# A linear-attention and token-mixer block: when one tile of h is normalised, and in what order GpSimd works

## The chip, the cores and the metric

The kernel runs on one core of one Trainium2 chip. The metric is the device time of one execution in microseconds (us), here 528.55 us as the median of three runs (527.94 to 528.89). Shorter is better. Engine names: TensorE (PE, matmuls and transposes; PEld is its weight load), VectorE (DVE), ScalarE (ACT), GpSimd (POOL) and SyncE (SP, which issues most DMAs).

## The reference

One sequence of S = 2048 tokens with D = 512 channels goes through two residual blocks. The first is a linear attention with 32 heads of 16 channels, the second a token-mixing MLP with F = 1792 hidden units.

```python
def _A_ref(x, wqkv, w_phi, wo):
    qkv = ((x @ wqkv).reshape(B, S, 3, H, Dh)).transpose(2, 0, 3, 1, 4)
    q, k, v = qkv[0], qkv[1], qkv[2]
    pq = einsum("bhsd,hdf->bhsf", q, w_phi)          # the same for pk
    phi_q = concatenate([softmax(pq), softmax(-pq)], -1)
    kv  = einsum("bhsf,bhsd->bhfd", phi_k, v);  z = einsum("bhsf->bhf", phi_k)
    num = einsum("bhqf,bhfd->bhqd", phi_q, kv)
    den = einsum("bhqf,bhf->bhq", phi_q, z)[..., None] + 1e-6
    return (num / den).transpose(0, 2, 1, 3).reshape(B, S, D) @ wo

def _B_ref(x, w1, b1, w2, b2):
    h = _layernorm(x)
    u = gelu(einsum("bsd,sf->bdf", h, w1) + b1)      # over the token axis
    return (einsum("bdf,fs->bds", u, w2) + b2).transpose(0, 2, 1)

h  = x + _A_ref(_layernorm(x), A_wqkv, A_w_phi, A_wo)
h2 = h + _B_ref(_layernorm(h), B_w1, B_b1, B_w2, B_b2)
```

## The kernel before

The tokens are cut into NT = 16 tiles of 128. Every large product is made of three fp32r matmuls (`mm3`, lines 63 to 67): high part by high part (L65), high by the low part of the moving operand (L66), low part of the weight by high (L67). So each operand is split into a high part, which ScalarE copies, and a low part, which a second engine subtracts (`split`, L58: copy at L60, subtraction at L61).

Up to about 140 us of the profile the keys, values and the sums over all tokens are made. Then comes the attention stage, the loop `for it in range(NT + 3)`. It is a software pipeline over the tiles: in iteration it each step works on a tile of its own. For PE, DVE, ACT and POOL the order of the instructions is the order in which the loop writes them, and each engine works its queue strictly in that order; SyncE's queue is ordered by a planner. The steps:

- `s_pq(t)` (GpSimd, L465): the product of the 128x1024 tile of query features with its weights; written in iteration t-1. TensorE's transposes of tile t need it.
- `s_ez(t)` (GpSimd, L447): the product ez of the features with the summed keys, in iteration t-3. `s_den` (VectorE, L456 to L462) makes the weights of the product from it.
- `negate` (GpSimd, L164, L165): the second half of a tile's logits, for ten tiles; the last of them comes around 182 us.
- `q_exp` (ScalarE, L176): the exponentials of a tile.
- `s_tr(t)` (TensorE, L532): eight transposes of tile t in iteration t; ScalarE copies them (`pht`, L534). There is one PSUM tile `tn` for them.
- `s_num(j)` (TensorE, L551): in even iterations, the numerator of the pair of tiles j = it/2-1 from `pht`, into the same `tn`; ScalarE copies its high part (`oh`, L557), VectorE subtracts the low part (`ol`, L562).
- `s_wo(t)` (TensorE): 12 matmuls into the single PSUM tile `po`, in iteration t+2. In even iterations it stands ahead of the transposes, in odd ones behind.
- `s_h(t)` (VectorE, L579): h = x + po and its row sums, at the end of iteration t+2; a DMA writes h out.
- `s_moments(t)` (ScalarE, L585 to L587): mean and variance of h, in iteration t+3.
- `s_rstd(t)` (GpSimd, L590 and L591): the root r2 = variance^-0.5 and then -mean times r2; in iteration t+3.
- `s_hn(t)` (ScalarE L595 and L60, GpSimd L61): the normalised tile hn = h * r2 + bias, its high part, and on GpSimd the low part of `hs`.
- `fill(p)` (TensorE, 6 matmuls `pu<-hs`): the MLP's first product for one tile of tokens and 256 hidden units. In iteration it it uses tile it-6 for p = 1, then tile it-5 for p = 0 (LAG = 5). Its weights are streamed: SyncE loads `wraw`, ScalarE makes `whi` (L614), VectorE `wlo` (L606, in `flush`).

`s_hn` is written in even iterations only, for two tiles: for tile it-4 near the head of the iteration, ahead of the exponentials and of `s_moments`, and for tile it-3 as the iteration's last step, behind `s_rstd(it-3)` of the same iteration.

After the loop come the rest of the MLP's first product (up to about 383 us) and its second product, both ordered for TensorE; from 255 us to the last product TensorE has no idle time in the profile.

Of the kernel before, what the change touches and what calls it, by code (L numbers as in the profile page):

```python
# [11 lines left out]
AF = mybir.ActivationFunctionType  # L12
# [7 lines left out]
NT = S // P  # L20
# [16 lines left out]
def block_kernel(ctx: ExitStack, tc: tile.TileContext, x, xT, wT, phic, wo, w1, b1, w2, b2,  # L37
                 kvmask, ident_in, out):
    nc = tc.nc
# [12 lines left out]
    r2 = cst.tile([P, NT], F32, name="r2")  # L52
# [5 lines left out]
    def split(hi, lo, src, lo_engine):  # L58

        nc.scalar.activation(hi, src, AF.Copy)  # L60
        lo_engine.tensor_sub(lo, src, hi)  # L61
# [98 lines left out]
    def negate():  # L160

        if MN:
            ev, mx, mn = MN.pop(0)
            nc.gpsimd.tensor_sub(mn, mn, mx)  # L164
            nc.gpsimd.tensor_sub(ev[:, :, 1], mn.unsqueeze(3).to_broadcast([P, NPR, 2, DH]), ev[:, :, 0])  # L165
# [5 lines left out]
    def run(*lists):  # L171
        for op in turns(*lists):
            op()
# [192 lines left out]
    def q_mm():  # L366
        if q["mm"] < NT:
            PS[q["mm"]] = proj(q["mm"], wqh, wql, ps_q, "pu")
            q["mm"] += 1

    def q_logits(lag):
        n = q["logits"]
        if n < min(NT, q["mm"] - lag + NT * (q["mm"] == NT)):
            EQ[n] = big.tile([P, NG, P], F32, name="eq", tag="big")
            q["logits"] += 1
            return logit_ops(PS[n], EQ[n], n >= len(Q_AT))
        return []

    def q_exp(lag):
        n = q["exp"]  # L380
        if n < min(NT, q["logits"] - len(MN) - lag):
            exps(n, EQ[n])
            q["exp"] += 1

    def q_sums(lag):
        n = q["sum"]
        if n < min(NT, q["exp"] - lag + NT * (q["exp"] == NT)):
            q["sum"] += 1
            return q_sum(n)
        return []  # L390
# [54 lines left out]
    def s_ez(t):  # L445
        EZ[t] = az.tile([P, NG, P], F32, name="ez")
        nc.gpsimd.tensor_mul(EZ[t], EQ[t], zB)  # L447

    def s_den(t):


        tz = az.tile([P, NPR, 2, 2], F32, name="tz")
        den = az.tile([P, NPR, 2], F32, name="den")
        W[t] = az.tile([P, NPR, 2, 2], F32, name="w", bufs=3)
        other = SQ[t]
        return [lambda: nc.vector.reduce_sum(tz.rearrange("p g c h -> p (g c h)"), heads(EZ[t]), axis=AX.X),  # L456
                lambda: nc.vector.scalar_tensor_tensor(tz[:, :, 0], other[:, :, 1], 1e-6, tz[:, :, 0],
                                                       op0=ALU.mult, op1=ALU.add),
                lambda: nc.vector.tensor_mul(tz, other, tz),
                lambda: nc.vector.reduce_sum(den, tz.rearrange("p g c h -> p g h c"), axis=AX.X),  # L460
                lambda: nc.vector.reciprocal(den, den),
                lambda: nc.vector.tensor_mul(W[t], other, den.unsqueeze(2).to_broadcast([P, NPR, 2, 2]))]  # L462

    def s_pq(t):
        nc.gpsimd.tensor_mul(heads(EQ[t]), heads(EQ[t]), W[t].rearrange("p g c h -> p (g c h)").unsqueeze(2).to_broadcast([P, 2 * H, DH]))  # L465
# [58 lines left out]
    HN, HT, PHT, OS, PO, VE = {}, {}, {}, {}, {}, {}  # L524

    def s_tr(t):
        j, i = divmod(t, 2)
        if i == 0:
            PHT[j] = ak.tile([P, NG, 2, P], F32, name="pht", bufs=1)
        ptr = ps_t.tile([P, 2, 4, P], F32, name="tn")  # L530
        for g in range(NG):
            nc.tensor.transpose(ptr[:, g // 4, g % 4, :], EQ[t][:, g, :], ident)  # L532
        for half in range(2):
            nc.scalar.activation(PHT[j][:, half * 4:half * 4 + 4, i, :], ptr[:, half], AF.Copy)  # L534

    def s_kv():

        pt = ps_o.tile([P, 2, P], F32, name="po")
        for b in range(2):
            nc.tensor.transpose(pt[:, b, :], kvS[:, 2 * b:2 * b + 2, :].rearrange("p n f -> p (n f)"), ident)  # L540
        nc.scalar.activation(kvB, pt, AF.Copy)

    def s_num(j):


        pn = ps_t.tile([P, 2, 4, P], F32, name="tn")
        for b in range(2):
            for c in range(4):
                for r in range(2):
                    rows, cols = slice(64 * r, 64 * r + 64), slice(32 * c, 32 * c + 32)  # L550
                    nc.tensor.matmul(pn[cols, r, 2 * b:2 * b + 2, :], kvB[rows, b, cols], PHT[j][rows, 4 * b + c, :, :],  # L551
                                     start=True, stop=True, skip_group_check=True)
        oh = ak.tile([P, 2, 2, 2, P], F32R, name="oh", bufs=1)
        ol = ak.tile([P, 2, 2, 2, P], F32R, name="ol", bufs=1)
        pv = pn.rearrange("p r (b i) s -> p i r b s", i=2)
        for i in range(2):
            nc.scalar.activation(oh[:, i], pv[:, i], AF.Copy)  # L557
        OS[j] = oh, ol, pv

    def s_ol(j):  # L560
        oh, ol, pv = OS[j]
        return [lambda i=i: nc.vector.tensor_sub(ol[:, i], pv[:, i], oh[:, i]) for i in range(2)]  # L562

    def s_wo(t):
        oh, ol, _ = OS[t // 2]
        i = t % 2
        PO[t] = po = ps_o.tile([P, D], F32, name="po")
        for j in range(4):
            mm3(po, oh[:, i, j // 2, j % 2, :], ol[:, i, j // 2, j % 2, :], woh[:, j, :], wol[:, j, :], j == 0, j == 3)

    def s_x(t):
        HT[t] = ak.tile([P, D], F32, name="h", bufs=4)
        nc.sync.dma_start(HT[t], x[t * P:(t + 1) * P, :])
# [8 lines left out]
    def s_moments(t):  # L582

        junk = ak.tile([P, D], F32, name="hj", bufs=1)
        nc.scalar.activation(VE[t][:, 1:2], VE[t][:, 2:3], AF.Copy, scale=-1.0 / D)  # L585
        nc.scalar.activation(junk, HT[t], AF.Square, bias=VE[t][:, 1:2], accum_out=VE[t][:, 3:4])
        nc.scalar.activation(VE[t][:, 0:1], VE[t][:, 3:4], AF.Identity, scale=(1.0 + EPS) / D, bias=eps2)  # L587

    def s_rstd(t):
        nc.gpsimd.tensor_tensor(r2[:, t:t + 1], VE[t][:, 0:1], mhalf[:, :1], op=ALU.pow)  # L590
        nc.gpsimd.tensor_mul(VE[t][:, 1:2], VE[t][:, 1:2], r2[:, t:t + 1])  # L591

    def s_hn(t):
        hn = ak.tile([P, D], F32, name="hn")
        nc.scalar.activation(hn, HT[t], AF.Identity, scale=r2[:, t:t + 1], bias=VE[t][:, 1:2])  # L595
        HN[t] = big.tile([P, 2, D], F32R, name="hs", tag="big")
        split(HN[t][:, 0], HN[t][:, 1], hn, nc.gpsimd)
# [5 lines left out]
    def flush():  # L603
        while LATER:
            wl_, raw, wh_ = LATER.pop(0)
            LO.append(nc.vector.tensor_sub(wl_, raw, wh_).ins)  # L606
# [35 lines left out]
    def fills(it):  # L642
        if FN[1] < it - LAG:
            fill(1, ps_q)
        if FN[0] <= it - LAG:
            fill(0, ps_f)

    for it in range(NT + 3):
        even = it % 2 == 0
        if 0 <= it + 1 < NT:  # L650
            s_pq(it + 1)
        if it == 0:
            s_tr(0)
            s_kv()
        if it == 1:
            run(q_logits(0))
            q_mm()
            s_tr(1)
        if it > 1 and even:
            if it <= NT:  # L660
                s_num(it // 2 - 1)
            if it >= 4:
                s_hn(it - 4)
        den = s_den(it + 2) if it + 2 < NT else []
        if it > 1 and even and it <= NT:
            ol = s_ol(it // 2 - 1)
            run(ol[:1] + den[:1] + ol[1:])
            den = den[1:]
        if it < NT:
            s_x(it)  # L670
        if it + 3 < NT:
            s_ez(it + 3)
        negate()
        q_mm()
        fills(it)
        q_exp(0)
        logits = q_logits(1)
        if it >= 3 and even:
            s_moments(it - 3)
        if it > 1 and even and it - 2 < NT:  # L680
            s_wo(it - 2)
        if 1 < it < NT:
            s_tr(it)
        if it > 1 and not even and it - 2 < NT:
            s_wo(it - 2)
        if it >= 3 and not even:
            s_moments(it - 3)
        if it >= 3:
            s_rstd(it - 3)
        run(logits + (q_sums(0) if it > 0 else []), den)  # L690
        flush()
        if 0 <= it - 2 < NT:
            s_h(it - 2)
        if it > 0:
            negate()
        if it >= 3 and even:
            s_hn(it - 3)
        for p in range(2):
            if it >= LAG - 3 + p and FL[p] <= FN[p] + 2 * (FN[p] > 0):
                fill_load(p)  # L700
# [139 lines left out]
    for n, (sp, p) in enumerate(STEPS):  # L840
        t = 2 * sp
# [118 lines left out]
```

## Time and profile before

| | |
|---|---|
| median of three runs | 528.55 us (527.94 to 528.89) |
| the profiled execution's own time | 527.88 us |
| its span, first to last instruction | 526.1 us |
| what lies around the span | 1.78 us |
| granted TensorE clock | 0.999 |
| busy: PE, PEld, DVE, ACT, POOL | 98%, 83%, 75%, 53%, 47% of the span |
| attention stage | about 140 to 256 us |

A row of the timeline gives the start and the duration in us, the engine, the source line, out<-in, and in brackets how long the engine was idle before it and which instruction ended the wait. Rows of repeated instructions are merged (x8). A row of the waits gives the total in us, the number of times, and the longest. A row of the windows gives a stretch and each engine's busy time in it, with the number of instructions in brackets. Durations on PE include the pipeline's depth: neighbouring matmuls overlap, so TensorE's pace is read from the distance of starts.

### The profile page before, as it was taken

The page shows a single profiled execution, that of the slowest core. Times are in us where ns is not written, and L with a number is a line of the kernel's source. Part 1 is how long each engine was busy: PE and PEld are TensorE (multiplying, and loading weights), DVE is VectorE, ACT ScalarE, POOL GpSimd, SP SyncE. Part 2 cuts the span into 40 slices and gives each one's busy share as a digit, 9 for nine tenths or more (in the row PEclk, how much of TensorE's full clock was granted, in tenths as well). Part 3 has the DMA queues.
Part 4 walks back from the last instruction along what each step waited for, and adds up shares of the span by engine and source line. Part 5 has one row for each costly group of instructions (what it writes and reads, how often), then busy time and mean ns, then how long its engine had stood idle before and what let it go on. Part 6 is the DMA issues. An engine that isn't in the chain of part 4 may idle for free.

```text
span 526.1 us, 8910 instructions
## 1 busy us (share of the span) xinstructions
PE 516.9 (98%) x3379; PEld 436.5 (83%) x3379; DVE 394.0 (75%) x681; ACT 277.7 (53%) x480; POOL 245.2 (47%) x204
## 2 busy tenths in 40 slices
PE   9999999999999979999999999999999999999997
PEld 8888888887877757777788888888889999999997
DVE  6893999976899989874426423824869889888985
ACT  6999843534247676557757422625553424444430
POOL 2589699985999988897425000000002122211210
PEclk9999999999999999999999999999999999999999
DMA  8634210020122233334234345532114686667733
GB/s 307 205 120 121 83 40 21 1 87 17 56 86 80 82 103 118 104 119 130 91 101 120 92 143 169 175 104 82 60 61 109 161 191 150 137 153 190 162 44 78
DMA packets 36298, 58.52 MB, mean 111 GB/s; under 512 B 3744, under 2 KB 19360, under 8 KB 36256
## 3 DMA queue, kind: packets, MB, share of 16 engines
q1 hardware_dynamic: 31936, 51.37, 30.4%
q0 software_dynamic: 4032, 6.42, 8.8%
q8 instruction: 26, 0.43, 0.3%
q10 hardware_dynamic: 288, 0.17, 0.1%
q14 instruction: 16, 0.13, 0.1%
HBM read 46.81 MB, written 11.14 MB: 110 GB/s over the span
## 4 chain that ended last, share of the span: by engine, by line
PE 82%; POOL 12%; DVE 3%; ACT 2%; issue 0%; POOLq 0%; ACTq 0%
PE py L822 11%; PE pu L65 11%; PE pu L66 10%; PE pu L67 10%; PE py L826 10%; PE py L823 6%; POOL ez L447 4%; POOL eq L465 3%; PE pv L66 3%; PE pv L67 3%; PE pv L65 3%; PE pk_ps L65 2%; PE pk_ps L66 2%; PE pk_ps L67 2%; POOL hs L61 2%; PE kvp L212 2%
## 5 line engine op out<-in xcount | busy, mean ns | idle before, releaser
L606 DVE TENSOR_TENSOR wlo<-wraw,whi 128x512 fp32r<-128x512 f32 x56 | 50.9, 912 | 56.2 <-ACT whi L614 56.0
L65 PE MATMUL pu<-hs,whi 128*128 128x512 f32 x224 | 87.2, 395 | 0.0
L66 PE MATMUL pu<-hs,whi 128*128 128x512 f32 x224 | 87.1, 389 | 0.0
L67 PE MATMUL pu<-hs,wlo 128*128 128x512 f32 x224 | 87.1, 390 | 0.0
L881 POOL DMA_DIRECT2D out<-ot x7 | 6.2, 889 | 157.3 <-DVE ot L877 157.3
L795 ACT ACTIVATE whi<-wraw 128x1792 fp32r<-128x1792 f32 x28 | 47.5, 1701 | 46.6 <-PE py L822 20.6
L804 DVE TENSOR_TENSOR wlo<-wraw,whi 128x1792 fp32r<-128x1792 f32 x28 | 56.5, 2022 | 12.5 <-PE py L823 8.9
L822 PE MATMUL py<-uf,whi 128*128 128x512 f32 x175 | 63.4, 399 | 0.0
L614 ACT ACTIVATE whi<-wraw 128x512 fp32r<-128x512 f32 x56 | 34.9, 626 | 50.3 <-PE pu L66 46.0
L65 PEld LDWEIGHTS pu<-hs,whi 128*128 128x128 f32 x224 | 42.1, 188 | 10.8 <-issue 2.5
L67 PEld LDWEIGHTS pu<-hs,wlo 128*128 128x128 f32 x224 | 42.1, 188 | 9.0 <-DVE wlo L606 0.4
L823 PE MATMUL py<-uf,wlo 128*128 128x256 f32 x175 | 49.2, 281 | 0.0
L66 PEld LDWEIGHTS pu<-hs,whi 128*128 128x128 f32 x224 | 42.1, 188 | 8.5
L447 POOL TENSOR_TENSOR ez<-eq,zB 128x1024 f32<-128x1024 f32 x16 | 40.6, 2539 | 4.4 <-ACT zB L494 4.4
L826 PE MATMUL py<-uf,whi 128*128 128x256 f32 x210 | 39.0, 283 | 0.0
L822 PEld LDWEIGHTS py<-uf,whi 128*128 128x128 f32 x175 | 33.0, 188 | 6.8
L200 POOL TENSOR_TENSOR pk<-pk,sk 128x1024 f32<-128x1024 f32 x16 | 31.0, 1940 | 7.6 <-DVE sk L199 5.0
L826 PEld LDWEIGHTS py<-uf,whi 128*128 128x128 f32 x210 | 32.4, 189 | 1.4
L823 PEld LDWEIGHTS py<-uf,wlo 128*128 128x128 f32 x175 | 33.1, 189 | 0.0
L465 POOL TENSOR_TENSOR eq<-eq,w 128x1024 f32<-128x1024 f32 x16 | 31.9, 1996 | 1.2 <-DVE w L462 1.2
L204 POOL TENSOR_TENSOR zacc<-zacc,pk 128x1024 f32<-128x1024 f32 x13 | 31.2, 2402 | 0.5
L61 POOL TENSOR_TENSOR hs<-hn,hs 128x512 fp32r<-128x512 f32 x16 | 21.4, 1340 | 17.9 <-ACT hs L60 17.9
(179 smaller groups left out, 1329.2 us busy)
## 6 DMA issues: line engine op xcount, KB each, us to landing
wraw<-in_w SPq DMA_DIRECT2D x56, 256.0 KB, 2.8
wraw<-in_w SPq DMA_DIRECT2D x28, 512.0 KB, 4.1
xraw<-in_xT SPq DMA_DIRECT2D x16, 256.0 KB, 2.9
xh<-in_x SPq DMA_DIRECT2D x16, 256.0 KB, 2.6
h<-in_x SPq DMA_DIRECT2D x16, 256.0 KB, 2.7
out<-h SPq DMA_DIRECT2D x16, 256.0 KB, 3.0
out<-ot POOLq DMA_DIRECT2D x14, 256.0 KB, 4.5
wraw<-in_wT SPq DMA_DIRECT2D x12, 256.0 KB, 4.9
```

The costliest lines, as they stand in the source:

```text
L65: nc.tensor.matmul(o, ah, bh, start=first, stop=False)
L66: nc.tensor.matmul(o, ah, bl, start=False, stop=False)
L67: nc.tensor.matmul(o, al, bh, start=False, stop=last)
L447: nc.gpsimd.tensor_mul(EZ[t], EQ[t], zB)
L465: nc.gpsimd.tensor_mul(heads(EQ[t]), heads(EQ[t]), W[t].rearrange("p g c h -> p (g c h)").unsqueeze(2).to_broadcast([P, 2 * H, DH]))
L606: LO.append(nc.vector.tensor_sub(wl_, raw, wh_).ins)
L614: nc.scalar.activation(wh_, raw, AF.Copy)
L795: nc.scalar.activation(WH[g], RAW[g], AF.Copy)
L804: nc.vector.tensor_sub(wl_, RAW[g], WH[g])
L822: nc.tensor.matmul(o, a[0], b, start=start, stop=stop, skip_group_check=True)
L823: nc.tensor.matmul(o[:, 0], a[1], b[:, 0], start=False, stop=stop, skip_group_check=True)
L826: nc.tensor.matmul(o[:, half], a[x], b[:, y], start=start and first and i == 0, stop=stop and i == 2, skip_group_check=True)
```

## The change

Four things are rewritten in the loop of the attention stage.

1. `s_hn` is written once in every iteration, always for tile it-4. On ScalarE it stands behind the exponentials and ahead of `s_moments(it-3)`; in odd iterations it stands behind `s_tr(it)`, so behind ScalarE's copies of the transposes. The loop has one more iteration (it = 19), in which tile 15 is normalised.
2. On GpSimd an iteration's order becomes product, ez, (negate), low part, root, (negate). Before, the low part stood ahead of ez for tile it-4, and at the end of the iteration, behind the root, for tile it-3.
3. The product of -mean and r2 (L591 on GpSimd) becomes an ACTIVATE of ScalarE on 128x1 elements, in front of hn.
4. While logits are still being made, `flush` (VectorE's `wlo`) stands behind `s_h` instead of ahead of it. Later it stays ahead.

The loads of h (`s_x`, four buffers) now wait for the later `s_hn` on ScalarE, and the planner puts SyncE's queue in a slightly different order. TensorE's matmuls are the same in number and, up to 13 tiles, in order; the last two fills of the loop are written in the added iteration.

```diff
     def s_rstd(t):
         nc.gpsimd.tensor_tensor(r2[:, t:t + 1], VE[t][:, 0:1], mhalf[:, :1], op=ALU.pow)
-        nc.gpsimd.tensor_mul(VE[t][:, 1:2], VE[t][:, 1:2], r2[:, t:t + 1])
 
     def s_hn(t):
+        nc.scalar.activation(VE[t][:, 1:2], VE[t][:, 1:2], AF.Copy, scale=r2[:, t:t + 1])
         hn = ak.tile([P, D], F32, name="hn")
...
-    for it in range(NT + 3):
+    for it in range(NT + 4):
...
-        if it > 1 and even:
-            if it <= NT:
-                s_num(it // 2 - 1)
-            if it >= 4:
-                s_hn(it - 4)
+        if it > 1 and even and it <= NT:
+            s_num(it // 2 - 1)
...
         logits = q_logits(1)
-        if it >= 3 and even:
+        if it >= 4 and even:
+            s_hn(it - 4)
+        if 3 <= it < NT + 3 and even:
             s_moments(it - 3)
...
-        if it >= 3 and not even:
+        if it >= 4 and not even:
+            s_hn(it - 4)
+        if 3 <= it < NT + 3 and not even:
             s_moments(it - 3)
-        if it >= 3:
+        if 3 <= it < NT + 3:
             s_rstd(it - 3)
         run(logits + (q_sums(0) if it > 0 else []), den)
-        flush()
+        if it > 0:
+            negate()
+        if not logits:
+            flush()
         if 0 <= it - 2 < NT:
             s_h(it - 2)
-        if it > 0:
-            negate()
-        if it >= 3 and even:
-            s_hn(it - 3)
+        flush()
```

## The prediction

> **What bounds the kernel now.** I read the page first, then TensorE's windows, then the waits of the attention stage, then the timeline of each engine around the places where TensorE stands still. The page:
>
> ```profile
> span 526.1 us, 8910 instructions
> PE 516.9 (98%) x3379; PEld 436.5 (83%) x3379; DVE 394.0 (75%) x681; ACT 277.7 (53%) x480; POOL 245.2 (47%) x204
> PE 82%; POOL 12%; DVE 3%; ACT 2%; issue 0%; POOLq 0%; ACTq 0%
> ```
>
> TensorE carries the kernel, but 12% of the chain that ended last (63 us) runs over GpSimd. Where does TensorE lose time? The windows (busy time of each engine in each stretch) show it; 260 to 270 us is a stretch at full pace, for comparison:
>
> ```profile
> 190.00:200.00 10.00, 7.23 (x60) 5.30 (x59) 8.82 (x14) 8.10 (x16) 8.29 (x7) 1.00 0.36 115
> 220.00:230.00 10.00, 9.18 (x67) 6.88 (x67) 8.74 (x17) 6.38 (x13) 8.25 (x8) 1.00 0.46 132
> 230.00:240.00 10.00, 8.93 (x76) 6.86 (x74) 7.76 (x18) 6.82 (x17) 8.33 (x7) 1.00 0.34 107
> 260.00:270.00 10.00, 10.00 (x46) 8.29 (x45) 4.34 (x8) 7.93 (x17) 4.08 (x6) 1.00 0.31 105
> ```
>
> Idle: 2.77, 0.82 and 1.07 us, 4.66 together. The clock is granted in full, so these are waits. By the starts on TensorE's timeline they are a little longer:
>
> ```profile
> 188.30 1.03 PE L532 MATMUL tn<-ident,eq 128*128 128x128 f32 x8
> 191.68 0.39 PE L67 MATMUL po<-woh,ol 128*128 128x512 f32 x1
> 194.84 1.10 PE L551 MATMUL tn<-pht,kvB 64*32 64x256 f32 x32 [2.77 <-ACT pht L534]
> 205.08 1.03 PE L532 MATMUL tn<-ident,eq 128*128 128x128 f32 x8
> 205.87 0.48 PE L65 MATMUL po<-woh,oh 128*128 128x512 f32 x1
> 208.81 1.10 PE L551 MATMUL tn<-pht,kvB 64*32 64x256 f32 x32
> 219.04 1.03 PE L532 MATMUL tn<-ident,eq 128*128 128x128 f32 x8
> 220.84 0.50 PE L65 MATMUL po<-woh,oh 128*128 128x512 f32 x1 [0.76 <-DVE h L579]
> 223.46 0.39 PE L67 MATMUL po<-woh,ol 128*128 128x512 f32 x1
> 223.91 1.10 PE L551 MATMUL tn<-pht,kvB 64*32 64x256 f32 x32
> 237.30 0.39 PE L66 MATMUL po<-wol,oh 128*128 128x512 f32 x1
> 237.52 0.39 PE L67 MATMUL po<-woh,ol 128*128 128x512 f32 x1
> 238.98 0.45 PE L551 MATMUL tn<-pht,kvB 64*32 64x256 f32 x8 [1.07 <-ACT pht L534]
> ```
>
> A matmul follows the one before by 0.22 to 0.23 us (237.30 to 237.52); eight transposes take 0.79 (205.08 to 205.87). So the losses are 3.16 - 0.23 = 2.93 us at iteration 8, 1.80 - 0.79 = 1.01 at iteration 11, 0.45 - 0.23 = 0.22 at iteration 12 and 1.46 - 0.23 = 1.23 at iteration 14: **5.4 us** in all. This is the most that the change can bring; TensorE's own work is the same in both kernels.
>
> Why does the numerator (L551) wait? The waits of the stage, and ScalarE's and GpSimd's timelines ahead of the first loss:
>
> ```profile
> ACT hn L595 <- POOL ve L591: 21.9, 11, 3.3
> POOL hs L61 <- ACT hs L60: 14.3, 8, 3.1
> ```
>
> ```profile
> 190.04 0.19 POOL L591 TENSOR_TENSOR ve<-ve,r 128x1 f32<-128x1 f32 x1
> 190.26 0.82 ACT L595 ACTIVATE hn<-h,ve,r 128x512 f32<-128x512 f32 x1 [3.30 <-POOL ve L591]
> 191.82 1.27 POOL L61 TENSOR_TENSOR hs<-hn,hs 128x512 fp32r<-128x512 f32 x1 [1.59 <-ACT hs L60]
> 193.73 1.06 ACT L534 ACTIVATE pht<-tn 128x512 f32<-128x512 f32 x2
> ```
>
> In iteration 6 the second `s_hn` makes ScalarE wait 3.30 us for GpSimd's root and product of the same iteration. Behind it in ScalarE's queue stand two weight copies, an exponential and the `pht` copies of iteration 7. TensorE's transposes for these were done at 188.30 + 0.79 = 189.1, but the copies start at 193.73. GpSimd in turn stands idle 1.59 us until ScalarE has made hn and hs. Two engines wait for each other in turn, and TensorE pays.
>
> **The change part by part.**
>
> *s_hn goes to the next iteration, behind the copies.* In odd iterations `pht` no longer stands behind hn. At iteration 8 the copies would start at 189.1 and end by about 190.5, before TensorE wants them at 191.9: 2.93 us gone. The same holds at iterations 12 and 14: 0.22 and 1.23 gone. The 1.01 us at iteration 11 is another wait: `po` is free only when VectorE has made h, and VectorE's weight subtraction in front of it was long:
>
> ```profile
> 217.23 2.39 POOL L447 TENSOR_TENSOR ez<-eq,zB 128x1024 f32<-128x1024 f32 x1
> 217.83 2.34 DVE L606 TENSOR_TENSOR wlo<-wraw,whi 128x512 fp32r<-128x512 f32 x1
> 219.58 1.00 POOL L590 TENSOR_TENSOR r<-ve,mhalf 128x1 f32<-128x1 f32 x1
> 220.09 0.68 DVE L579 SCALAR_TENSOR_TENSOR h<-po,h 128x512 f32<-128x512 f32 x1
> ```
>
> `wlo` ends at 220.17, 0.55 us behind ez (219.62), and the root behind ez takes 1.00 us: a VectorE subtraction with two SBUF inputs seems to wait for the GpSimd instruction that runs, and holds up the next one. [...] In the changed kernel GpSimd makes ez one iteration ahead of VectorE's need and ahead of the low part, so VectorE's chain starts sooner, and `wlo` with it; I count this loss as gone too.
>
> *The product on ScalarE.* ScalarE gets 16 small ACTIVATEs. The nearest row is its 128x1 Copy at L585:
>
> ```profile
> L585 ACT ACTIVATE ve<-ve 128x1 f32<-128x1 f32 x16 | 3.1, 193 | 1.2 <-DVE h L579 1.2
> L590 POOL TENSOR_TENSOR r<-ve,mhalf 128x1 f32<-128x1 f32 x16 | 9.7, 604 | 4.7 <-ACT ve L587 4.7
> ```
>
> 16 x 0.19 = 3.1 us on an engine that is busy 53%; on the path to the low part it costs 0.2 each, nothing while that path has slack (below). GpSimd saves from 0.14 to 0.65 us an iteration, as the rows below show.
>
> *The low part behind ez.* This is the cost. The low part of tile t must be there before the second matmul of fill p = 0 in iteration t+5. The tight place is iteration 7 (tile 2), because GpSimd is late there after ten negations:
>
> ```profile
> 165.47 0.65 POOL L591 TENSOR_TENSOR ve<-ve,r 128x1 f32<-128x1 f32 x1
> 173.54 0.69 POOL L591 TENSOR_TENSOR ve<-ve,r 128x1 f32<-128x1 f32 x1
> 175.83 1.30 POOL L61 TENSOR_TENSOR hs<-hn,hs 128x512 fp32r<-128x512 f32 x1 [0.25 <-ACT hs L60]
> 181.98 0.19 POOL L591 TENSOR_TENSOR ve<-ve,r 128x1 f32<-128x1 f32 x1
> 183.47 1.94 POOL L465 TENSOR_TENSOR eq<-eq,w 128x1024 f32<-128x1024 f32 x1
> 185.37 1.29 POOL L61 TENSOR_TENSOR hs<-hn,hs 128x512 fp32r<-128x512 f32 x1
> 186.63 2.83 POOL L447 TENSOR_TENSOR ez<-eq,zB 128x1024 f32<-128x1024 f32 x1
> 186.92 0.39 PE L66 MATMUL pu<-hs,whi 128*128 128x512 f32 x1
> ```
>
> Today the low part of tile 2 ends at 186.66 and TensorE takes it at 186.92. In the changed order GpSimd reaches that point without three L591 (0.65, 0.69 and 0.19 us) and without the 0.25 us wait, so 1.78 us sooner; tiles 0 and 1 only swap places with their ez. But ez comes first now, 2.4 us, or 2.8 if a `wlo` falls into it. The low part then runs from 185.37 - 1.78 + 2.4 = 186.0 (186.4) to 187.3 (187.7). TensorE waits 0.4 to 0.8 us at iteration 7, nothing if GpSimd gains another small wait, 1.3 if one more collision of 0.45 us falls into the earlier steps. I take 0.7.
>
> *Iteration 8.* Root 0.6, product 1.9 and ez 2.4 to 2.8 bring GpSimd to 192.3 to 193.1. ScalarE: transposes end at 189.1 + 0.7 = 189.8, `pht` by 191.0, the small product (0.2), and hn and hs (190.26 to 191.82 above, 1.56) by 192.8. So the low part of tile 3 ends at 194.1 to 194.4. TensorE starts the iteration at 191.9 + 0.7 = 192.6 and needs it after the numerator (1.03), one fill (6 x 0.23) and a first matmul, at 195.3. No wait.
>
> *From there on* the longest loop goes from the end of an odd iteration's transposes: `pht` 1.15, small product, hn and hs 1.8, low part 1.3, root 0.6 (the moments of 1.3 behind hs are just done), product 1.9, ez 2.4, low part 1.3: 10.5 us, up to 11.8 with three collisions of 0.45. TensorE wants that low part after 12 matmuls (12 x 0.227 = 2.72), numerator 1.1, two fills (2.8), 12 matmuls (2.72), transposes 0.79, one fill and a matmul (1.6): 11.7 us. It fits by 1.2 us, or just not. GpSimd's own work for a pair of tiles is 2 x (1.9 + 2.4 + 1.3 + 0.6) = 12.4 us, up to 13.8 if every ez, root and product is stretched; TensorE's pair takes 13.97 (194.84 to 208.81) with no long wait in it. GpSimd bounds the stage today because of the bubbles (1.59 us a pair and more), and no longer does without them.
>
> *The rest.* `flush` behind `s_h` frees `po` and ScalarE's input sooner while logits are made; TensorE loses nothing there today, so nothing is counted. The load of h for tile t now waits for hn of tile t-4 in iteration t; VectorE wants it at the end of iteration t+2, some 14 us on, and SyncE's queue behind it holds weight loads that are wanted over an iteration later: nothing. The added iteration: tile 15's low part is wanted behind fills of other tiles in both kernels; TensorE has no idle time there today, and the chain is h, moments, root, hn, low part, about 6 us, against seven fills of 1.36 us: nothing.
>
> *The sum.* 5.4 - 0.7 = **4.7 us** off the span: 526.1 to 521.4, 527.88 to 523.2 for the profiled execution, whose time is 0.67 us under the median. For the median, 528.55 - 4.7 = **523.9 us**.
>
> [...]
>
> **The rivals.**
>
> *A, the slack is eaten.* Each collision adds 0.45 us (ez 2.83 against 2.39, the root 1.00 against 0.55). If most iterations take three and a semaphore's delay at each hand-over, the low part comes 0.3 to 0.8 us late in each of four pairs (iterations 7 to 14): 1.2 to 3.2 more. Time 525.1 to 527.1. For it: GpSimd and VectorE get denser. Against: the loop has room in most cases.
>
> *B, the h of VectorE.* With GpSimd never idle every `wlo` meets a running instruction and holds h and `po`. If each of four odd iterations loses the 1.0 us that iteration 11 loses now, the gain is 4.7 - 4 = 0.7, or 2.7 if half of them do. Time 525.9 to 527.9. [...]
>
> *C, slower: the low part stays late.* ez in front of the low part costs 2.4 to 2.8 us in the first iterations; if GpSimd gains none of it back (product and root wait for VectorE and ScalarE as they do now), TensorE waits 2.1 + 0.5 = 2.6 at iteration 7, and GpSimd stays the bound with 15.1 us a pair (208.81 to 223.91) against 13.97, so 0.6 an iteration over eight iterations. 2.6 + 4.8 = 7.4 against 5.4: 530.5. It decides if the new waits exceed 5.4 us. Against it: the rows above show where the 1.78 us come from.
>
> *D, nothing moves.* TensorE reaches the long fills sooner and meets loads or VectorE's `wlo` there. Against: from 260 to 270 us, where such fills run at full pace, DMA is busy 0.31 and VectorE 4.34 of 10 us. Time 528.5.
>
> **How the numbers follow.** A change under 0.2% (1.1 us) can't be told from none here. Forecast 0.56, gain 3.9 to 5.4 and a little more if smaller waits go too: 522.9 to 524.7. A 0.14, B 0.08, C 0.14, D 0.08. Faster 0.78 (forecast, A, B), same 0.08, slower 0.14. The range 522.8 to 527.6 leaves out C and D.
>
> **What would show it.** Right: no PE wait for `pht` and none of 0.8 us for h; hn on ScalarE waiting little for GpSimd; the low parts behind ez; one short wait of the fill at about 187 us; numerators about 13.9 us apart. Wrong: fills `pu<-hs` that wait for `hs` L61 in iteration after iteration (A, C), `po` for h (B), or idle time past 255 us (D).

## The result, and the profile after

The changed kernel takes 524.15 us (median; 523.96 to 524.46) against 528.43 us, **4.28 us or 0.8% less**; the ratio to the kernel before is 0.992 (95% interval 0.9902 to 0.9937). The forecast was 523.9 us, in a range of 522.8 to 527.6. The profiled execution took 524.12 us with a span of 522.3 us, 3.8 us under the span before.

The page of the changed kernel, the lines that answer to those of before:

```profile
span 522.3 us, 8917 instructions
PE 516.6 (99%) x3379; PEld 436.5 (84%) x3379; DVE 386.5 (74%) x681; ACT 282.3 (54%) x496; POOL 239.8 (46%) x188
PE 90%; POOL 7%; DVE 2%; issue 1%; ACT 0%; POOLq 0%
```

TensorE's busy time is the same (516.9 and 516.6), so what went is idle time. GpSimd's share of the chain that ended last went from 12% to 7%. The windows that had idle time, and the one at full pace:

```profile
190.00:200.00 10.00, 10.00 (x76) 7.74 (x74) 8.32 (x16) 8.24 (x19) 9.51 (x6) 1.00 0.48 145
220.00:230.00 10.00, 10.00 (x77) 7.74 (x76) 7.26 (x17) 7.98 (x19) 8.68 (x8) 1.00 0.34 106
230.00:240.00 10.00, 10.00 (x77) 7.73 (x75) 5.51 (x14) 7.76 (x19) 5.56 (x5) 1.00 0.40 133
260.00:270.00 10.00, 10.00 (x45) 8.26 (x44) 3.10 (x5) 5.17 (x11) 3.14 (x3) 1.00 0.36 107
```

The 2.77, 0.82 and 1.07 us of idle time are gone. The waits of the stage (engine, what waited, what ended it, total us, times, longest):

```profile
ACT pht L534 <- PE tn L532: 30.2, 16, 4.3
POOL hs L61 <- ACT hs L60: 21.2, 9, 7.6
PE pu L66 <- POOL hs L61: 1.2, 1, 1.2
```

ScalarE's 21.9 us of waits for GpSimd's L591 have disappeared; its waits for TensorE's transposes grew from 15.4 to 30.2 us, as they should on an engine beside the bound. GpSimd still waits for ScalarE's hs, for longer than before (21.2 against 14.3 us), but that is slack: nobody is late for it. One wait of TensorE's is left. The timeline of TensorE shows it, and the starts of the numerators behind it:

```profile
186.91 0.39 PE L65 MATMUL pu<-hs,whi 128*128 128x512 f32 x1
188.46 0.50 PE L66 MATMUL pu<-hs,whi 128*128 128x512 f32 x1 [1.16 <-POOL hs L61]
...
193.16 0.39 PE L67 MATMUL po<-woh,ol 128*128 128x512 f32 x1
193.48 1.09 PE L551 MATMUL tn<-pht,kvB 64*32 64x256 f32 x32
207.39 1.09 PE L551 MATMUL tn<-pht,kvB 64*32 64x256 f32 x32
221.30 1.09 PE L551 MATMUL tn<-pht,kvB 64*32 64x256 f32 x32
235.22 1.09 PE L551 MATMUL tn<-pht,kvB 64*32 64x256 f32 x32
```

At iteration 7 the second matmul of the fill starts 1.55 us after the first instead of 0.23: a wait of 1.32 us for the low part of tile 2. After that the numerators follow each other by 13.91, 13.91 and 13.92 us: TensorE's own pace. From the last numerators to the end both kernels take the same 273.2 us (526.1 - 252.91 before, 522.3 - 249.13 after), so the whole difference lies in the attention stage.

### The profile page after: what moved, and what is told of

Read it like the earlier page. It is cut to its first block, busy times and chain, and to the rows that moved or that the text cites. A ratio compares the mean times of both kernels' runs of the same rounds, so it can differ in the third digit from the quotient of the medians.

```text
span 522.3 us, 8917 instructions
## 1 busy us (share of the span) xinstructions
PE 516.6 (99%) x3379; PEld 436.5 (84%) x3379; DVE 386.5 (74%) x681; ACT 282.3 (54%) x496; POOL 239.8 (46%) x188
## 4 chain that ended last, share of the span: by engine, by line
PE 90%; POOL 7%; DVE 2%; issue 1%; ACT 0%; POOLq 0%
PE pu L65 12%; PE pu L66 12%; PE pu L67 11%; PE py L823 11%; PE py L827 10%; PE py L824 6%; PE pv L66 3%; PE pv L67 3%; PE pv L65 3%; PE pk_ps L65 2%; PE pk_ps L67 2%; PE pk_ps L66 2%; POOL ez L447 2%; POOL eq L465 2%; PE po L67 2%; PE po L65 2%
## 5 line engine op out<-in xcount | busy, mean ns | idle before, releaser
L606 DVE TENSOR_TENSOR wlo<-wraw,whi 128x512 fp32r<-128x512 f32 x56 | 43.8, 784 | 53.2 <-ACT whi L614 53.0
L447 POOL TENSOR_TENSOR ez<-eq,zB 128x1024 f32<-128x1024 f32 x16 | 38.4, 2400 | 4.4 <-ACT zB L494 4.4
L534 ACT ACTIVATE pht<-tn 128x512 f32<-128x512 f32 x32 | 17.4, 596 | 30.2 <-PE tn L532 30.2
```

## The experiments

All times below are medians; the kernel before ran beside each group on the same chip (527.77 to 528.33 us), so ratios are the safer comparison. Profiled executions start the first transposes of the attention stage at 140.3 to 141.3 us; this is noise of some tenths in every span.

**Which part brings the gain.** Two parts were taken back and one was done alone.

```diff
# e1: the small product on GpSimd again
     def s_rstd(t):
+        nc.gpsimd.tensor_mul(VE[t][:, 1:2], VE[t][:, 1:2], r2[:, t:t + 1])
     def s_hn(t):
-        nc.scalar.activation(VE[t][:, 1:2], VE[t][:, 1:2], AF.Copy, scale=r2[:, t:t + 1])
# e6: hn ahead of the copies in odd iterations
+        if it >= 4 and not even:
+            s_hn(it - 4)
         if 1 < it < NT:
             s_tr(it)
...
-        if it >= 4 and not even:
-            s_hn(it - 4)
# e7: the kernel before, with the small product alone on ScalarE (e1's edit the other way round)
```

> The changed kernel with the small product (-mean times root) back on GpSimd, in its old place behind the root; the rest of the change stays. Theory (GpSimd's lateness counts only at iteration 7; later TensorE is the bound and has slack): three more instructions of 0.14 to 0.19 us ahead of the low part of tile 2, so TensorE's wait at iteration 7 grows from 1.4 to 1.8 to 2.0 us; time 524.5 to 524.8. Rival (the product matters in every iteration, GpSimd is still the bound): 13 times 0.2 us, 526.7 or more.

Measured: 525.38 us, ratio 0.9953 (0.9941 to 0.9966). The wait at iteration 7 grew to 1.59 us, by less than expected (1.8 to 2.0), but three more came: 0.36 and 0.32 us at iterations 5 and 6, and 0.67 at iteration 8, where the fill waits for the weights' low part. I had looked at one tight place; the early iterations are all tight, and each 0.15 to 0.2 us on GpSimd is paid several times there. The rival (a price in every iteration to the end) did not happen either: past iteration 8 there is no wait.

> The kernel before with only the small product moved from GpSimd to ScalarE. Theory (the wait of the two engines for each other stays as it is): GpSimd's 0.19 us become ScalarE's 0.29 on the same path, TensorE still waits some 3 us at iteration 8; 528.0 to 528.8 against 528.4 before, no change that can be told. Rival (GpSimd's load is what bounds the stage, so a relief of it is worth something alone): 1 to 2 us less, 526.5.

Measured: 526.86 us, ratio 0.9982 (0.9973 to 0.9991). The wait for `pht` stays, as the theory said, but it is shorter: TensorE's losses at iterations 8, 11 and 14 are 2.76, 0.72 and 1.07 us against 2.93, 1.01 and 1.23, 0.6 us less. The theory's "no change" missed; where GpSimd is the bound, 0.2 us less on it an iteration is worth something, 0.9 us by the medians (0.5 to 1.4 by the interval).

> The changed kernel with hn ahead of ScalarE's copies of the transposes in odd iterations too. Theory (the gain comes from taking the root of the iteration before, not from the place behind the copies): the root of tile 3 ends at 188.9, the copies of iteration 7 begin at 190.8, so hn fits in between in most iterations; numerators wait 0 to 0.3 us, time 523.9 to 524.6. Rival (the place behind the copies is what brings the gain): numerators wait again by 1 us or more at iterations 8, 12 and 14, 526 to 527.

Measured: 524.42 us, ratio 0.9935 (0.9923 to 0.9947). No numerator waits. The wait at iteration 7 is the same (1.31), and one of 0.45 us for the weights' low part comes at iteration 8. So the gain is not from the place behind the copies: what is left is that hn uses a root of the iteration before, which is ready when ScalarE comes to it (in e6 ScalarE waits for a root once in the stage, 0.3 us). The low part behind ez on GpSimd does not bring it either: in e3 below it stands ahead, and no numerator waits there. The reverse of e6, the place behind the copies with a root of the same iteration, was not run.

**What is left at iteration 7.** GpSimd's timeline of the changed kernel up to the wait:

```profile
166.78 2.39 POOL L465 TENSOR_TENSOR eq<-eq,w 128x1024 f32<-128x1024 f32 x1
174.62 2.39 POOL L465 TENSOR_TENSOR eq<-eq,w 128x1024 f32<-128x1024 f32 x1
182.44 1.94 POOL L465 TENSOR_TENSOR eq<-eq,w 128x1024 f32<-128x1024 f32 x1
184.34 2.38 POOL L447 TENSOR_TENSOR ez<-eq,zB 128x1024 f32<-128x1024 f32 x1
186.69 1.72 POOL L61 TENSOR_TENSOR hs<-hn,hs 128x512 fp32r<-128x512 f32 x1
```

Two products of 2.39 us instead of 1.94 and a low part of 1.72 instead of 1.29: three times 0.45. VectorE's weight subtraction stands beside each:

```profile
166.06 1.31 DVE L606 TENSOR_TENSOR wlo<-wraw,whi 128x512 fp32r<-128x512 f32 x1
174.19 1.02 DVE L606 TENSOR_TENSOR wlo<-wraw,whi 128x512 fp32r<-128x512 f32 x1
186.22 1.05 DVE L606 TENSOR_TENSOR wlo<-wraw,whi 128x512 fp32r<-128x512 f32 x1
```

Two experiments ask whether these collisions are the cause, and whether the new place of the subtraction behind h made them.

```diff
# e4: the first four subtractions become a memset
+            if len(LO) < 4:
+                LO.append(nc.vector.memset(wl_.bitcast(F32), 0.0).ins)
+                continue
             LO.append(nc.vector.tensor_sub(wl_, raw, wh_).ins)
# e2: the subtraction always ahead of h
-        if not logits:
-            flush()
+        flush()
         if 0 <= it - 2 < NT:
             s_h(it - 2)
-        flush()
```

> The changed kernel with the low parts of the first four streamed weight blocks set to zero by VectorE instead of subtracted from two tiles (their part of the MLP's first product is left out). Theory (collisions of these subtractions with GpSimd put the low part of tile 2 late): product of tile 5, product of tile 6 and low part of tile 2 last 1.94, 1.94 and 1.30 us instead of 2.39, 2.39 and 1.72; the low part of tile 2 ends at 187.0 instead of 188.4 and TensorE's wait at iteration 7 falls from 1.4 to 0.2 us or less; time 522.8 to 523.2. Rival (GpSimd's own work makes it late): 524.1.

Measured: 522.5 us, ratio 0.9895 (0.9882 to 0.9909). GpSimd's rows:

```profile
166.29 1.94 POOL L465 TENSOR_TENSOR eq<-eq,w 128x1024 f32<-128x1024 f32 x1
173.66 1.94 POOL L465 TENSOR_TENSOR eq<-eq,w 128x1024 f32<-128x1024 f32 x1
185.31 1.29 POOL L61 TENSOR_TENSOR hs<-hn,hs 128x512 fp32r<-128x512 f32 x1
```

All three are short, the low part of tile 2 ends at 186.6, and TensorE's wait falls to 0.36 us. The collisions are the cause of about 1 us of the wait. The median is 1.7 us under the changed kernel's: the profiled execution also came to the stage 0.5 us sooner (140.35 against 140.85), and the rest is not traced.

> The changed kernel with VectorE's weight subtraction always ahead of h again, as before the change. Theory (the subtraction meets a running GpSimd instruction wherever it is put, and costs GpSimd 0.45 us each time): the two stretched products (2.39 us) of iterations 4 and 5 become 1.94, but the root or the negation beside the earlier subtraction is stretched instead; wait at iteration 7 and time within 0.3 us of the changed kernel's, 523.8 to 524.5. Rival (the new place of the subtraction made two collisions that were not there before): both go, the wait falls from 1.4 to 0.5 us, 523.2.

Measured: 523.97 us, ratio 0.9924 (0.9911 to 0.9938), not to be told from the changed kernel. The wait at iteration 7 fell to 0.60 us, because the first subtraction now stretches a negation by 0.33 instead of a product by 0.45, but another came. Windowed timeline at iteration 5:

```profile
173.32 1.50 DVE L606 TENSOR_TENSOR wlo<-wraw,whi 128x512 fp32r<-128x512 f32 x1
174.74 0.68 DVE L579 SCALAR_TENSOR_TENSOR h<-po,h 128x512 f32<-128x512 f32 x1
175.49 0.50 PE L65 MATMUL po<-woh,oh 128*128 128x512 f32 x1 [0.72 <-DVE h L579]
```

The subtraction waits behind a negation, h behind the subtraction, and TensorE for `po`: 0.96 us by the starts. This is rival B of the prediction in one place. So the subtraction behind h is neither better nor worse in sum: it moves the collision.

**Putting the low part ahead of ez.** If ez in front makes the low part late, why not swap them, in iteration 6 alone or everywhere?

```diff
# e8 (iteration 6 alone; e3 does it in every iteration)
-        if it + 3 < NT:
+        if it + 3 < NT and it != 6:
             s_ez(it + 3)
...
+        if it == 6:
+            s_ez(it + 3)
         if 3 <= it < NT + 3:
             s_rstd(it - 3)
# e9, e9b: e8, and the weight subtraction of iterations 6 and 7 ahead of VectorE's denominators;
# e10: this alone; e11: as e9, this subtraction early in every iteration from 6 on
+        if it in (6, 7):
+            flush()
         run(logits + (q_sums(0) if it > 0 else []), den)
```

> The changed kernel with GpSimd's order in iteration 6 alone changed: low part of tile 2 ahead of ez of tile 9. Theory (only the place of ez there makes the fill of iteration 7 wait): the low part starts 2.4 us sooner, at 184.3, and ends by 186.0, ahead of the fill at 186.9; the wait of 1.4 us goes, ez of tile 9 ends at 188.0, when VectorE is just ready for it; time 522.7. Rival (the wait is only passed on: ez later makes VectorE's weights and the next low parts later): wait of 0.5 to 1.4 us at iteration 8 or 9, 523.2 to 524.1.

Measured: 524.48 us, ratio 0.9933 (0.9919 to 0.9946): nothing won. The low part is early (184.29 to 185.57), but the fill now waits one matmul later, for the other low part. Timelines of VectorE and TensorE:

```profile
186.19 2.30 DVE L606 TENSOR_TENSOR wlo<-wraw,whi 128x512 fp32r<-128x512 f32 x1
188.54 0.50 PE L67 MATMUL pu<-hs,wlo 128*128 128x512 f32 x1 [1.06 <-DVE wlo L606]
195.46 0.50 PE L67 MATMUL pu<-hs,wlo 128*128 128x512 f32 x1 [0.43 <-DVE wlo L606]
```

VectorE's subtraction starts while GpSimd's ez runs (185.53 to 187.93 here), lasts 2.30 us instead of the 1.05 of the changed kernel, and ends at 188.49, 0.56 us behind ez. My theory had overlooked it; the rival was right that the wait is passed on, but not by the way it named.

> The changed kernel with the low part ahead of ez on GpSimd in every iteration (product, low part, ez, root). Theory (whatever stands behind ez is late, and with the low part in front it is VectorE's weight subtraction, which waits for ez to end): no wait of the fill for GpSimd's low part, but a wait of 1 us or so for the weights' low part at iteration 7, and in odd iterations GpSimd waits some 2.5 to 3 us for ScalarE's hs ahead of ez, which its slack bears; time 524 to 525.5. Rival (GpSimd's waits for ScalarE make it the bound again): a loss in every pair of iterations, 526 to 528.

Measured: 527.61 us, ratio 0.9993 (0.9984 to 1.0002): the whole gain is lost. It is the theory's mechanism, at three times its size and an iteration later than expected (iteration 7 loses 0.24 us): at iteration 8 two subtractions in a row last 4.19 us, until 196.74, 0.54 us behind ez (193.40 to 196.20).

```profile
192.55 4.19 DVE L606 TENSOR_TENSOR wlo<-wraw,whi 128x512 fp32r<-128x512 f32 x2
196.80 0.50 PE L67 MATMUL pu<-hs,wlo 128*128 128x512 f32 x1 [3.10 <-DVE wlo L606]
```

TensorE's starts there are 3.50 us apart, a loss of 3.27. Behind it the matmuls follow each other by 0.43 us instead of 0.23 for some 3 us (see the last section). GpSimd's waits for ScalarE, the rival, reach 5.49 us (ahead of 211 us), and TensorE does not wait behind them.

> The changed kernel with the low part ahead of ez in iteration 6, and VectorE's weight subtractions of iterations 6 and 7 ahead of the rest of its denominators. Theory (the fill of iteration 7 waits for the later of two low parts, the one behind ez; both must come ahead of it): the weight subtraction runs behind the product, about 184.4 to 185.0, the low part of tile 2 ends by 186.5, ez after both; no wait over 0.3 us at iterations 7 and 8; time 522.6 to 523.0. Rival (the delay comes out elsewhere: VectorE's weights for the product are 1.4 us later, h too): waits for po or for the product's transposes of 0.5 to 1.5 us, 523.5 to 524.5.

Measured: 523.01 us, ratio 0.9905 (0.989 to 0.992). No wait at iteration 7; one of 0.30 us at iteration 8. To set it against the changed kernel on one chip:

> The changed kernel itself, beside the next three on one chip. Theory: as measured, 4.0 to 4.5 us under the kernel before, with one wait of about 1.4 us at iteration 7 and none elsewhere. Rival (its place on the chip or the start of its loads moved it): another wait, or a difference beyond 1 us.

> Low part ahead of ez in iteration 6 and VectorE's weight subtractions of iterations 6 and 7 early, again, beside the changed kernel. Theory (the wait at iteration 7 is all that is left to win): 1.0 to 1.4 us under the changed kernel. Rival (its lower time was the chip's): within 0.3 us of it.

> The changed kernel with VectorE's weight subtractions of iterations 6 and 7 early, and ez ahead of the low part as in the changed kernel. Theory (the fill waits for what stands behind ez, here the low part): the subtraction now collides with the product instead of the low part, so the low part of tile 2 lasts 1.3 instead of 1.7 us but starts 0.45 us later; the wait at iteration 7 stays, 1.2 to 1.6 us, time within 0.3 us of the changed kernel's. Rival (the subtraction alone makes the low part late): the wait falls below 0.8 us, 0.6 us or more under the changed kernel.

> As the kernel with both low parts early, but with VectorE's weight subtraction early in every iteration from 6 on. Theory (from iteration 8 on everything has slack, TensorE is the bound): no difference to it beyond 0.3 us. Rival (VectorE's denominators, made later by each subtraction, hold up GpSimd's product or h): 0.5 us or more slower than it.

| | us (lowest to highest) | ratio to before (95%) | TensorE's wait at iteration 7 |
|---|---|---|---|
| a1, the changed kernel | 524.22 (524.04 to 524.70) | 0.9923 (0.9910 to 0.9937) | 1.32 |
| e10, subtraction early | 523.67 (523.65 to 524.65) | 0.9918 (0.9905 to 0.9932) | 1.33 |
| e9b, both low parts early | 523.30 (522.85 to 523.51) | 0.9903 (0.9890 to 0.9917) | none |
| e11, as e9b, the subtraction early from iteration 6 on | 523.03 (522.81 to 523.60) | 0.9901 (0.9888 to 0.9915) | none |

e10 keeps the wait at the same size, as expected: its subtraction stretches ez to 2.85 us instead of the low part to 1.7. Only with both low parts ahead of ez is the wait gone, and the time is some 1 us under the changed kernel's: the runs of e9b and e11 all lie below all of a1's, though the intervals of the ratios overlap. e11 and e9b can't be told apart. They are the best versions here that leave nothing out.

## Why the prediction was right, step by step

- *5.4 us of TensorE's waits go.* Right, all four: the three windows are full, and no numerator and no `po` waits. The size is 0.3 us too large: ahead of a numerator I took off 0.23 us for a matmul, but without a wait the step is 0.32 (193.16 to 193.48), so the four losses are 2.84, 1.01, 0.13 and 1.14, 5.1 us in all. e6 corrects the reason I gave by half: what matters is the root from the iteration before, not the place behind the copies.
- *One new wait at iteration 7, 0.7 us.* Right in place and cause, too small: 1.32 us. The mis-sized term is the 1.78 us that I let GpSimd gain. I counted L591 at its durations of 0.65, 0.69 and 0.19 us, but the first two were a small product of 0.19 and a collision of some 0.45 with VectorE's subtraction. Taking the small product away didn't take the collision away; it went to the next instruction, the product of 2.39 us. By the starts the gain was 1.03 us: ez starts at 184.34, where the low part started at 185.37. The third collision, on the low part itself, was in my bound ("1.3 if one more collision falls into the earlier steps").
- *The small product on ScalarE costs nothing and saves GpSimd a little.* It takes 0.29 us and not 0.19 on ScalarE, which has the time. Its worth was underrated: 0.9 us alone (e7), and within the change (e1) 1.2 us by the medians and 1.6 by TensorE's waits (2.94 against 1.32).
- *From iteration 8 on it fits.* Right: 13.91 us a pair; the loop's slack was enough even with collisions.
- *Flush, loads of h, the added iteration: nothing.* Right in sum. The flush is not free of effect (e2), its two effects cancel.
- *The sum.* 5.1 - 1.3 = 3.8 us of waits, which is what the span lost (526.1 to 522.3); 4.7 was predicted, so both terms erred in favour of the change. The medians differ by 4.28 us because the four executions of the kernel before lie between 527.94 and 528.89 and the profiled one was the shortest (the last section has a likely reason). That the time came within 0.3 us of the forecast is in part luck: 0.5 us of the gain is in none of the forecast's terms.
- *The rivals.* A and B each exist in one place (iteration 7; iteration 5 of e2). C needed the low part to be late for eight iterations; it was late for one. D did not show: TensorE has no wait past 189 us.

The swap of iteration 6 was misjudged in e8: I followed one of the fill's two low parts and not the other.

## What to carry to other kernels

When two engines wait for each other within one iteration, let the one use a value that the other made an iteration earlier; where it stands in its queue then mattered little here (e6). Before crediting the removal of an instruction with its duration, ask how much of it is its own: a 128x1 product that takes 0.65 us once and 0.19 another time carries somebody else's wait, and that stays. And follow every operand of the instruction that waits: with one made early, the next one is the last to come.

## What the runs showed of the hardware

**A subtraction on VectorE and GpSimd's instructions beside it lengthened each other.** VectorE's 128x512 subtraction from two SBUF tiles lasted 0.68 us with GpSimd idle (at 232.46 us in the changed kernel). Where it started while a GpSimd instruction ran, it ended 0.5 to 0.6 us behind that one in the timelines of the kernel before, the changed kernel, e2, e3, e8 and e9, and lasted up to 2.34 us (217.83 us in the kernel before). The GpSimd instruction that followed at once lasted some 0.45 us longer in most of these rows: product 2.39 instead of 1.94, low part 1.72 instead of 1.29 (changed kernel), ez 2.85 instead of 2.40 (e10), root 1.00 instead of 0.55 (kernel before). A memset in its place left the two products at 1.94 us and the low part at 1.29 (e4). VectorE's subtraction at L562, with one operand in PSUM, kept its 0.69 us beside a running product (167.44 us in the changed kernel).

**In e3 the clock was lower behind a wait of 3.3 us.** After 3.10 us of idle time on TensorE, the windows show the granted clock (the third column from the end) at 0.57 between 197 and 201 us:

```profile
193.00:197.00 4.00, 0.90 (x9) 0.47 (x4) 4.00 (x3) 1.81 (x5) 4.00 (x3) 1.00 0.35 109
197.00:201.00 4.00, 4.00 (x11) 3.14 (x11) 3.93 (x8) 2.94 (x7) 3.99 (x4) 0.57 0.62 182
201.00:204.00 3.00, 3.00 (x17) 2.50 (x16) 2.40 (x7) 0.00 (x0) 3.00 (x3) 1.00 0.05 20
```

Against 1.00 that is 0.43 x 4 = 1.7 us of the four. By the starts on TensorE's timeline, the eight matmuls from 197.37 us on take 3.38 us (the ninth starts at 200.75) instead of 8 x 0.23 = 1.84, 1.5 us more. So my estimate is 1.5 to 1.7 us lost beside the wait. Of e3's twelve executions the one with a mean clock of 1.00 was the shortest, 526.47 us against 526.98 to 528.68.

The 2.77 us of idle time in the kernel before left the clock at 1.00 in the profiled execution. Other executions of it, of which only the time and the mean clock are on record, look different. Beside e3, 7 of its 23 had a mean clock of 0.992 to 0.994 and took 528.64 to 528.87 us; the other 16, at 0.997 or more, took 527.38 to 528.43. The kernel of e7, with 2.61 us of idle time, had such a clock in 2 of 12 executions. In the 48 executions of the changed kernel and of the experiments whose longest wait in the stage is 1.6 us or less, the clock was never under 0.999. So the long waits of the kernel before may cost it clock too in some executions, and the change would end that. No trace of such an execution is on record, so this is argued and not shown, and it is open which waits go with a lower clock.
